# One pool of PSUM banks, pairs of 64 rows for the linear part and the sums, more queries turned by DMA

## The chip, the core and the metric

The kernel runs on one core of one Trainium2 chip. The core has five engines with a queue each: TensorE (PE, with PEld for its weight loads), VectorE (DVE), ScalarE (ACT), GpSimd (POOL) and SyncE (SP), which here issues almost all DMA transfers. An engine takes its queue in order. Matmuls write to PSUM, which has eight banks of 128 x 512 fp32; the other data lie in SBUF. The metric is the device time in microseconds of one execution; lower is better.

## What is computed

Attention through 49 agents, and a maxout layer behind it, in fp32 at the outside:

```python
B, N, C = (4, 12544, 128); n_agents = 49; d_ff = 768
def sm(a, b):
    s = scale * (a @ b.transpose(0, 2, 1))
    s = s - s.max(-1, keepdims=True)
    e = np.exp(s)
    return e / (e.sum(-1, keepdims=True) + 1e-09)
a2k = sm(agents, k)
agent_v = a2k @ v
q2a = sm(q, agents)
x = (q2a @ agent_v).reshape(B * N, C)
h = np.maximum(np.maximum(x @ w1, x @ w2), x @ w3)
out = h @ w_out
```

## The kernel before, in words

The kernel never forms x. For each batch b it works out `G` = agent_v times (w3-w1), (w2-w1) and (w1 w_out): 49 rows, kept twice, at partitions 0 to 48 and 64 to 112. The maximum of three products is then w1's product plus what two rectified differences add, and w1's product goes through the output layer as one linear part.

The queries come in 49 groups of 1024 (the last one takes two tiles of each batch). Steps have names, with the group s in them:

- `ql.s`, `qc.s`: SP loads q, POOL casts it to bf16. Then q is turned, either by `qt.s` (eight transposes on PE into PSUM) and `qe.s` (DVE copies that to SBUF), or by `qd.s` (one transposing DMA on SP). The set `TURNED` says which groups use `qd`.
- `sc.s`, `ex.s`: scores against the agents (two matmuls of 64 columns of the array each), and ACT's exponential, `e.s`: two halves of 49 rows, for even and odd tiles.
- `su.s`, `re.s`: PE sums the exponentials, DVE takes the reciprocals.
- for each of six parts f of the hidden layer: `u.s.f` and `v.s.f` on PE (two matmuls of 49 rows each, one per half, side by side in the array), `a.s.f` on ACT (relu of u), `x.s.f` on DVE (maximum of v and a, into `r`). For f = 4 ACT does both.
- `li.s.o`: the linear part of output tile o, opening its bank; `p.s.o.f`: four matmuls per part f and output tile o; `ov.s.o` on DVE scales by the reciprocals; `st.s` on SP stores.

For batches 1 to 3 the keys and values come in 11 chunks each, worked off between the query groups, about one a group until group 33: `kl`, `vl` load, `kc`, `vc` cast on POOL, `kt` turns by DMA, `ks` and `kx` make scores and exponentials, `kv` the weighted sum, `va` adds up. Batch 0 is done ahead of group 0, and there PE turns the keys.

The order of all steps is written out in the table `ORDER`, and `run` issues them in that order; each engine's queue follows from it. A number behind a name gives the place of its tile. PSUM is divided in two: `UV`, three tiles of two banks, for u, v and the early work; and `OM`, two tiles of one bank, for the turned q, the scores, the sums, the K chunks and the output tiles. The waits are placed by the framework.

In the profile L558 is u and v, L571, L565 and L568 are ACT's relus, L574 is DVE's maximum, L592 is p, L582 is li, L545 is su, L533 is sc, L523 is qt, L527 is qe, L599 is ov, L454 is every transposing DMA, L359 and L376 are ks and kv.

## Time and profile before

| | us |
|---|---|
| median of 3 runs (451.83 to 452.58) | 452.12 |
| profiled execution, span from first to last instruction | 449.8 |
| PE, DVE, ACT, POOL busy in it | 423.7, 402.8, 395.1, 169.4 |
| first hidden matmul (u of group 0) | 42.0 |

The profiled execution's own time beyond its span isn't given; the median of the runs lies 2.3 us over the span. Busy times are sums of records, and records of one engine overlap: matmuls flow through the array behind one another, and a busy engine isn't one at its limit. A row of a group has its line, engine, operation, tiles, shapes and count, then busy time and mean ns of one, then the idle time ahead of it. A tile mode, below, is the shape in which the array is used: all 128 rows, two halves of 64 rows, or two halves of 64 columns.

### The profile page before, as it was taken

The numbers are of one execution on the slowest core, as the hardware profiler recorded it, in microseconds if no ns is written. First come the engines' busy times: TensorE is split into PE (matmuls) and PEld (weight loads), VectorE is DVE, ScalarE is ACT, GpSimd is POOL, SyncE is SP. The second block draws the span as 40 slices with busy tenths as digits, with TensorE's granted clock in tenths as the row PEclk, the third lists the DMA queues.
The fourth block names the chain that finished last, engine by engine and source line by source line (L and its number), as shares of the span: only waits on it lengthen the run. The fifth ranks groups of instructions, "written<-read, shape, count | busy, mean of one in ns | idle before, by whom it ended". The sixth has DMA issues, their size and how long they took to land.

```text
span 449.8 us, 13103 instructions
## 1 busy us (share of the span) xinstructions
PE 423.7 (94%) x5388; PEld 274.0 (61%) x5388; DVE 402.8 (90%) x512; ACT 395.1 (88%) x461; POOL 169.4 (38%) x176
## 2 busy tenths in 40 slices
PE   0778899999999999999999999999999999999996
PEld 0654466666665666666666666666666655565675
DVE  1335999999999999999999999999999999999986
ACT  1459999999988999999989999999889899999983
POOL 1641645455676372464363263453402110100000
PEclk9989999999999999999999999999999999999999
DMA  8999999999999998999969799498608685327142
GB/s 311 409 408 387 326 373 310 263 394 316 340 320 274 392 216 223 408 273 318 406 200 324 216 350 226 141 314 336 212 6 230 191 221 129 96 103 178 48 177 107
DMA packets 80150, 117.80 MB, mean 262 GB/s; under 512 B 53527, under 2 KB 56283, under 8 KB 80091
## 3 DMA queue, kind: packets, MB, share of 16 engines
q1 hardware_dynamic: 79888, 116.87, 83.6%
q8 instruction: 42, 0.69, 0.6%
q14 instruction: 17, 0.14, 0.1%
q10 hardware_dynamic: 203, 0.10, 0.1%
HBM read 78.74 MB, written 25.69 MB: 232 GB/s over the span
## 4 chain that ended last, share of the span: by engine, by line
PE 73%; DMA 12%; DVE 6%; POOL 2%; ACT 2%; SPq 2%; issue 2%; POOLq 0%; DVEq 0%
PE UV L558 29%; PE OM L592 27%; DMA LD<-in_k_dram 6%; PE OM L582 5%; DMA LD<-in_v_dram 4%; DVE R L574 4%; PE OM L523 3%; PE OM L533 3%; PE OM L376 2%; DMA out_dram<-OS 2%; PE OM L359 2%; DVE OS L599 1%; SPq L454 1%; ACT AS L571 1%; ACT VB L333 1%
## 5 line engine op out<-in xcount | busy, mean ns | idle before, releaser
L574 DVE TENSOR_TENSOR R<-UV,AS 128x1024 bf16<-128x1024 f32 x245 | 293.4, 1219 | 11.4 <-PE UV L558 5.3
L571 ACT ACTIVATE AS<-UV 128x1024 bf16<-128x1024 f32 x245 | 246.7, 1023 | 18.3 <-PE UV L558 11.7
L558 PE MATMUL UV<-EQ,G 49*128 49x512 bf16 (+1 forms) x1248 | 178.5, 368 | 2.1 <-DVE R L574 1.3
L592 PE MATMUL OM<-wo_bf,R 128*128 128x128 bf16 x2352 | 179.8, 219 | 0.0
L592 PEld LDWEIGHTS <-R 128*128 128x128 bf16 x2352 | 139.7, 98 | 39.5 <-issue 37.3
L558 PEld LDWEIGHTS <-G 49*128 49x128 bf16 x1248 | 58.7, 93 | 63.9 <-issue 23.8
L517 POOL CAST QB<-LD 128x1024 bf16<-128x1024 f32 x49 | 50.8, 1040 | 111.9 <-DMA LD<-in_q_dram 50.6
L599 DVE TENSOR_TENSOR OS<-OM,RC 128x512 f32<-128x512 f32 x98 | 67.3, 686 | 2.6 <-PE OM L592 1.4
L335 POOL CAST KB<-LD 128x1152 bf16<-128x1152 f32 (+2 forms) x45 | 49.7, 1116 | 40.6 <-DMA LD<-in_k_dram 35.9
L335 POOL CAST VB<-LD 128x1152 bf16<-128x1152 f32 (+1 forms) x33 | 37.3, 1137 | 40.4 <-DMA LD<-in_v_dram 24.3
L568 ACT ACTIVATE R<-UV 128x1024 bf16<-128x1024 f32 x49 | 50.1, 1022 | 2.5 <-PE UV L558 1.7
L565 ACT ACTIVATE UV<-UV 128x1024 f32<-128x1024 f32 x49 | 49.9, 1019 | 2.3 <-DVE R L574 1.2
L582 PE MATMUL OM<-G,EQ 128*128 128x256 bf16 x196 | 37.9, 275 | 0.0
L474 POOL TENSOR_TENSOR EA<-EA,EK 128x441 f32<-128x441 f32 x27 | 27.6, 1023 | 18.5 <-ACT EK L365 18.1
L539 ACT ACTIVATE EQ<-OM 128x512 bf16<-128x512 f32 x49 | 29.4, 601 | 1.0 <-PE OM L533 0.9
L527 DVE COPY QT<-OM 128x1024 bf16<-128x1024 bf16 x38 | 26.0, 684 | 1.1 <-PE OM L523 1.0
L347 DVE COPY KT<-UV 128x1152 bf16<-128x1152 bf16 (+1 forms) x12 | 8.2, 700 | 18.2 <-PE UV L342 18.2
L523 PE MATMUL OM<-ident,QB 128*128 128x128 bf16 x304 | 23.7, 222 | 0.6 <-POOL QB L517 0.6
L582 PEld LDWEIGHTS <-EQ 128*128 128x128 bf16 x196 | 12.3, 97 | 15.9 <-issue 15.2
L523 PEld LDWEIGHTS <-QB 128*128 128x128 bf16 x304 | 18.5, 99 | 4.3 <-issue 2.6
L359 PEld LDWEIGHTS <-KT 128*128 128x128 bf16 x392 | 14.3, 98 | 10.0 <-issue 5.5
L533 PE MATMUL OM<-QT,agT 128*64 128x512 bf16 (+1 forms) x104 | 20.2, 393 | 0.0
(67 smaller groups left out, 196.4 us busy)
## 6 DMA issues: line engine op xcount, KB each, us to landing
LD<-in_q_dram SPq DMA_DIRECT2D x48, 512.0 KB, 6.6
out_dram<-OS SPq DMA_DIRECT2D x48, 512.0 KB, 6.3
LD<-in_k_dram SPq DMA_DIRECT2D x40, 576.0 KB, 7.8
LD<-in_v_dram SPq DMA_DIRECT2D x40, 576.0 KB, 9.4
LD<-in_k_dram SPq DMA_DIRECT2D x3, 512.0 KB, 6.0
LD<-in_v_dram SPq DMA_DIRECT2D x3, 512.0 KB, 11.4
LD<-in_moe_w_dram SPq DMA_DIRECT2D x6, 192.0 KB, 8.4
KT<-KB SPq DMA_TRANSPOSE x33, 6.7
```

What stands on the lines that cost most here:

```text
L335: (self.nc.gpsimd if eng == POOL else self.nc.vector).tensor_copy(out=out, in_=src)
L517: return lambda: self.nc.gpsimd.tensor_copy(out=self.t[f"qb.{s}"], in_=self.t[f"q.{s}"][:, :GT, :])
L523: self.nc.tensor.transpose(t[:, j * P:(j + 1) * P], self.t[f"qb.{s}"][:, j, :], self.ident)
L533: self.nc.tensor.matmul(self.t[f"qs.{s}"][h * H:(h + 1) * H, jj * P:(jj + pairs) * P], self.agT[:, b, :], self.t[f"qT.{s}"][:, 2 * jj + h: ...
L558: self.nc.tensor.matmul(t[:, h, jj * P:(jj + pairs) * P], self.t[f"G{b}"][h * H:h * H + A, c + f * P:c + (f + 1) * P], self.t[f"e.{s}"][h ...
L565: return lambda: self.nc.scalar.activation(self.t[f"u.{s}.{f}"], self.t[f"u.{s}.{f}"], AF.Relu)
L568: return lambda: self.nc.scalar.activation(self.t[f"r.{s}.{f}"], self.t[f"u.{s}.{f}"], AF.Relu)
L571: return lambda: self.nc.scalar.activation(self.t[f"a.{s}.{f}"], self.t[f"u.{s}.{f}"], AF.Relu)
L574: return lambda: self.nc.vector.tensor_tensor(out=self.t[f"r.{s}.{f}"], in0=self.t[f"v.{s}.{f}"], in1=self.t[f"a.{s}.{f}"], op=ALU.max)
L582: self.nc.tensor.matmul(self.t[f"o.{s}.{o}"][:, i * 2 * C:(i + 1) * 2 * C], self.t[f"e.{s}"][:, jj * P:(jj + 1) * P], self.t[f"G{of[jj]}"] ...
L592: self.nc.tensor.matmul(self.t[f"o.{s}.{o}"][:, c:c + C], self.t[f"r.{s}.{f}"][:, h, jj * P:(jj + 1) * P], self.wo_bf[:, f, :], start=Fals ...
L599: self.nc.vector.tensor_tensor(out=self.t[f"os.{s}"][:, j:j + 4, :], in0=self.t[f"o.{s}.{o}"].rearrange("p (j c) -> p j c", c=C), in1=self ...
```

## The change

1. PSUM is one pool `PS` of eight banks. A tile of u or v takes any two banks with a fixed distance (also 2 and 3, or 4 and 5), the others one bank.
2. Output tile o holds the tiles of parity o instead of the first or the last four, so that `p.s.o.f` reads one half of `r` alone. The tiles are opened by whichever step comes first, and the order fills one and then, mostly, the other.
3. The linear part `li.s` is one step of eight matmuls: the two halves of 49 rows side by side, each into its own output tile. `G` loses 128 columns of zeros for that. The sums are two steps `su.s.0` and `su.s.1`, of 49 rows and one column each; the second waits until the first has ended, as both write one bank.
4. `TURNED` has 22 groups instead of 11: 22, 25, 28 and 30 to 48.
5. The order is new, with another rule for the waits: the kernel works out itself which semaphores a step must wait for (`Plan.waits`), leaves out what an earlier wait implies, and puts all but one of a step's waits into instructions of their own. A helper records all instructions, so the changed kernel's rows all stand under L377. Steps `kr`, `fo.i` and `rs0` are parts of former steps, and the products for G come in halves of 384 columns.

Mode changes of the array, counted over PE's whole order: 569 before, 620 after. Instructions that only wait: on ACT 357 and 63, on DVE 309 and 133, on PE 6 and 100.

```diff
-C31, C21, C1O, WC = 0, DFF, 2 * DFF, 2 * DFF + 2 * C
+C31, C21, C1O, WC = 0, DFF, 2 * DFF, 2 * DFF + C
-TURNED = range(38, 49)
+TURNED = (22, 25, 28, *range(30, 49))
-SLOTS = {"UV": 3, "OM": 2, "LD": 13, "QB": 3, "KB": 3, "VB": 4, "KT": 3, "QT": 3, "EQ": 4, "EK": 4, "AS": 3,
+SLOTS = {"PS": 8, "LD": 13, "QB": 3, "KB": 3, "VB": 4, "KT": 3, "QT": 3, "EQ": 4, "EK": 4, "AS": 3,
...
-        add(f"su.{s}", PE, em.sums(s, m, not h), mm(GT // 2, 2), after=[f"ex.{s}"] + ([f"ks{b}.{g}" for b in range(1, B)
+        su = plan.tile("PS", f"su.{s}")
+        for h in range(2):
+            add(f"su.{s}.{h}", PE, em.sums(s, h), mm(GT // 2, 1), mode=ROW, after=[f"ex.{s}", "ones"], use=[su, f"e.{s}"], sides={su: h}, half=h)
...
-            add(f"li.{s}.{o}", PE, em.out_linear(s, o), mm(2, 256), after=[f"ex.{s}"] + lin, new=[("OM", f"o.{s}.{o}")], use=[f"e.{s}"] + gs)
+        add(f"li.{s}", PE, em.out_linear(s), mm(4, 128), mode=ROW, after=[f"ex.{s}"] + lin, use=both + [f"e.{s}"] + gs, sides=straight)
+                    add(f"p.{s}.{o}.{f}", PE, em.out_hidden(s, o, f), mm(4, 128), after=made[s, f][o] + ["cwo"], use=[both[o], f"r.{s}.{f}"])
...
+    def sums(self, s, h):
+        def fn():
+            t, rows = self.t[f"su.{s}"], slice(h * H, h * H + A)
+            for jj in range(GT // 2):
+                c = 4 * h + jj
+                self.nc.tensor.matmul(t[:, c:c + 1], self.t[f"e.{s}"][rows, jj * P:(jj + 1) * P], self.ones_bf[rows, :1],
+                                      start=self.first[f"su.{s}"] == self.now and jj == 0, stop=True, skip_group_check=True)
+        return fn
...
+    def out_linear(self, s):
+        def fn():
+            of = [p[0] for p in parts_of(s) for _ in range(p[4])]
+            for jj in range(GT // 2):
+                for h in range(2):
+                    rows = slice(h * H, h * H + A)
+                    self.nc.tensor.matmul(self.t[f"o.{s}.{h}"][:, jj * C:(jj + 1) * C], self.t[f"e.{s}"][rows, jj * P:(jj + 1) * P],
+                                          self.t[f"G{of[jj]}"][rows, C1O:], start=self.opens(s, h) and jj == 0, stop=True,
+                                          skip_group_check=True)
+        return fn
+
+    def out_hidden(self, s, o, f):
+        def fn():
+            for jj in range(GT // 2):
+                self.nc.tensor.matmul(self.t[f"o.{s}.{o}"][:, jj * C:(jj + 1) * C], self.t[f"r.{s}.{f}"][:, o, jj * P:(jj + 1) * P],
+                                      self.wo_bf[:, f, :], start=self.opens(s, o) and jj == 0, stop=True, skip_group_check=True)
+        return fn
...
+    def run(self, plan, order, place, tc):
...
+        waits, told, at, self.first = plan.waits(order, place)
+        for name in order:
+            o = plan.ops[plan.index[name]]
+            for x in waits[name][:-1]:
+                who, value = mark[x]
+                self.queues[o["eng"]].wait_ge(sems[who], value)
+            made.clear()
+            self.now = name
+            o["fn"]()
+            for x in waits[name][-1:]:
+                who, value = mark[x]
+                made[0].wait_op(sems[who], value, "sem-ge")
...
-kl0.5/0 prep kl0.0/1 kl0.9/2 kl0.1/3 kl0.6/4 vl0.0/5 vl0.11/6 ql.0/7 kl0.2/8 kl0.10/9 kl0.7/10 kc0.1/0 vl0.5/11 kc0.9/1 kt0.1/0
+kl0.11/12 kl0.10/0 agl id0 ql.0/1 qc.0/1 kl0.6/2 kl0.9/3 ones agc kc0.10/2 id kc0.6/0 kl0.4/8 kl0.2/1 agt/4 vl0.4/4 prep
```

PE's queue in the middle of the program, where a K chunk, the sums of one group and the linear part of the group ahead of it stand together. EQ is `e`, G0 the products of batch 0, R7 a tile of `r`; `sel` picks the two halves. Before, each load of weights is a row of its own:

```order
L359 MATMUL OM1_2715<-agT_77,KT2_2365 128x49
L545 LDWEIGHTS EQ0_2702
L545 MATMUL OM1_2715<-sel_79,EQ0_2702 128x2
...
L582 LDWEIGHTS EQ1_2317
L582 MATMUL OM0_2729<-G0_646,EQ1_2317 128x256
...
L592 LDWEIGHTS R7_2573
L592 MATMUL OM0_2729<-wo_bf_86,R7_2573 128x128
```

All of it uses the array at full height. After, a matmul and its load are one row, `x4` counts equal rows, and ps is the pool:

```order
L377 MATMUL ps_76<-QT1_104,agT_69 64x512 x2
L377 MATMUL ps_76<-wo_bf_72,R12_129 128x128 x4
L377 MATMUL ps_76<-ones_bf_66,EQ2_108 128x1 x4
L377 MATMUL ps_76<-EQ2_108,G1_144 128x512 x2
L377 MATMUL ps_76<-ones_bf_66,EQ2_108 128x1 x4
L377 MATMUL ps_76<-EQ2_108,G1_144 128x512 x4
L377 MATMUL ps_76<-G1_144,EQ1_107 128x128 x8
L377 MATMUL ps_76<-wo_bf_72,R8_125 128x128 x4
```

The two halves of the sums now stand on both sides of one hidden pair, and the linear part (128x128 x8) at the end of a run of hidden pairs, in their tile mode.

DVE's queue around group 30, where the first of the consecutive newly turned groups is used. Before:

```order
L465 TENSOR_TENSOR VA_4904<-OM_5876,VA_4904 128x49
L550 RECIPROCAL RC_5947<-OM_5876 128x8
L599 TENSOR_TENSOR OS_5852<-OM_5869,RC_5595 128x512
L574 TENSOR_TENSOR R_5965<-UV_5955,AS_5932 128x1024
L527 COPY QT_5992<-OM_5976 128x1024
L574 TENSOR_TENSOR R_6005<-UV_5998,AS_5906 128x1024
```

After, in the same place:

```order
L377 RECIPROCAL RC_130<-ps 128x8
L377 TENSOR_TENSOR R_121<-ps,AS_116 128x1024
L377 TENSOR_TENSOR OS_134<-ps,RC_132 128x4x128
L377 TENSOR_TENSOR R_120<-ps,AS_114 128x1024
L377 TENSOR_TENSOR VA_147<-ps,VA_147 128x49
L377 TENSOR_TENSOR OS_134<-ps,RC_132 128x4x128
```

The copy of the turned q is gone; maxima, scalings, sums and reciprocals remain.

SP's queue where the last K chunks of batch 3 are turned. Before:

```order
L454 DMA_TRANSPOSE KT_5775<-KB_5748 128x9x128
L325 DMA LD_5807<-in_k_dram 128x1024
L513 DMA LD_5814<-in_q_dram 128x1024
L513 DMA LD_5823<-in_q_dram 128x1024
L325 DMA LD_5835<-in_v_dram 128x1152
L454 DMA_TRANSPOSE KT_5847<-KB_5649 128x9x128
```

After:

```order
L377 DMA_TRANSPOSE KT_102<-KB_93 128x9x128
L377 DMA_TRANSPOSE QT_103<-QB_90 128x8x128
L377 DMA_TRANSPOSE KT_101<-KB_94 128x9x128
L377 DMA_TRANSPOSE QT_105<-QB_91 128x8x128
L377 DMA out_dram<-OS_142 128x1024
L377 DMA_TRANSPOSE QT_104<-QB_90 128x8x128
```

Transposes of q stand between those of K, and loads and stores behind them.

More of the change, by code (lines that the diff above doesn't have):

```diff
@@ L76, in parts_of, with lane @@
+    def lane(self, o, place, first):
+        if not o["use"]:
+            return "AG"
+        t = [x for x in o["use"] if first[x] == o["name"]] or o["use"]
+        cls = self.tiles[t[0]]
+        return f"{cls}{place[t[0]][0]}" + ("b" if cls == "LD" and first[t[0]] != o["name"] else "")
 def parts_of(s):
@@ L96, in mm @@
     t = n * max(cols / 2400 + 0.0025, 0.0253)
-    return t, t + 0.235
+    return t, t + 0.2
 def act(cols):
@@ L200, in graph @@
-        add(f"nr{b}", DVE, em.normalise(b, m), (0.5, 0.62), after=[f"to{b}", f"va{r}"], new=[("KR", f"kr{b}"), ("G", f"G{b}")],
-            use=[m, f"va{b}"], bank=m)
-        for name, c0, c1, eng in (("a", C31, C31 + DFF, ACT), ("c", C21, C21 + DFF, DVE), ("l", C1O, WC, ACT)):
+            use=[m, f"es{b}", f"e{r}"])
+        held = [f"gp{x}" for x in "abcd"] + ["gl"] if b == 2 else [f"gp{x}{b - 2}" for x in "abcdl"] if b > 2 else []
+        add(f"kr{b}", DVE, em.reciprocal_of(b, m), (0.25, 0.3), after=[f"to{b}"], new=[("KR", f"kr{b}")], use=[m])
@@ new lines, in graph @@
+            if f != FI:
+                for z, h in halves["v"]:
+                    v = f"v.{s}.{f}{z}"
+                    two = (1.136, 1.26) if h is None else (0.6, 0.72)
+                    add(v, PE, em.hidden(v, s, f, C21, True, h), pe, mode=ROW, after=[f"ex.{s}"] + needs("c", "d"),
+                        new=[("PS", v, 3 if h is None else 1)], use=[e] + gs, half=h)
+                    add(f"x.{s}.{f}{z}", DVE, em.max_second(v, s, f, h), two,
+                        after=[v] + [f"a.{s}.{f}{y}" for y, i in halves["u"] if i is None or h is None or i == h],
+                        use=[v, f"a.{s}.{f}", plan.tile("R", f"r.{s}.{f}")])
@@ L286, in __init__ @@
         self.w1T = const.tile([P, NF, P], BF16, name="w1T")
[L287 to L294 removed]
+        self.wall = const.tile([P, WC], BF16, name="wall")
+        self.ps = pools["psum"].tile([P, SLOTS["PS"], 512], FP32, name="ps")
```

812 lines of the change are left out of this document (458 added, 354 removed).

## The prediction

> **What bounds the kernel now.** I read the engines' shares first, then the busy time by stage, then the chain of work by stage, and last the order of TensorE in time, because a share near 100% says little on an engine whose matmuls overlap.
>
> ```profile
> span 449.8 us, 13103 instructions
> PE 423.7 (94%) x5388; PEld 274.0 (61%) x5388; DVE 402.8 (90%) x512; ACT 395.1 (88%) x461; POOL 169.4 (38%) x176
> ```
>
> Three engines look almost equally full. The table by stage (columns: stretch, its length, busy time of PE, weight loads, DVE, ACT, POOL, clock, DMA share, GB/s) doesn't part them either:
>
> ```profile
> 60.00:150.00 90.00, 88.43 (x1160) 57.43 (x1157) 85.60 (x109) 82.49 (x98) 52.37 (x53) 1.00 1.09 328
> 240.00:330.00 90.00, 89.99 (x1198) 59.02 (x1195) 88.17 (x113) 85.23 (x101) 38.47 (x40) 1.00 0.81 247
> 330.00:360.00 30.00, 29.74 (x334) 18.32 (x331) 29.26 (x34) 27.43 (x33) 5.20 (x5) 1.00 0.56 161
> 360.00:430.00 70.00, 69.71 (x744) 40.22 (x743) 67.09 (x74) 67.32 (x75) 5.17 (x5) 1.00 0.51 139
> ```
>
> DVE's 88.17 of 90 us is too high a reading: three maxima in a row took 3.49 us as one run, 1.16 each, while a single one has 1.219 in its group, so the records overlap by some 0.06 to 0.08 us each.
>
> ```profile
> 199.18 3.49 DVE L574 TENSOR_TENSOR R<-UV,AS 128x1024 bf16<-128x1024 f32 x3
> L574 DVE TENSOR_TENSOR R<-UV,AS 128x1024 bf16<-128x1024 f32 x245 | 293.4, 1219 | 11.4 <-PE UV L558 5.3
> L527 DVE COPY QT<-OM 128x1024 bf16<-128x1024 bf16 x38 | 26.0, 684 | 1.1 <-PE OM L523 1.0
> ```
>
> The chain of work decides it. From 240 to 330 us it is PE and nothing else; from 360 to 430 us, where q comes turned by DMA, some 13% of it lies on DVE, ACT and issue.
>
> ```profile
> by line: PE UV L558 38.8%; PE OM L592 35.6%; PE OM L582 7.1%; PE OM L523 5.8%; PE OM L533 4.1%; PE OM L376 3.8%; PE OM L359 3.2%; PE OM L545 1.2%; PE OM L491 0.3%; PE OM L493 0.2%; issue 0.0%
> by line: PE UV L558 40.3%; PE OM L592 34.3%; DVE R L574 6.9%; PE OM L582 6.5%; PE OM L533 4.3%; ACT AS L571 3.0%; issue 2.1%; DVE OS L599 1.6%; PE OM L545 1.4%; DVEq L574 0.0%
> ```
>
> So PE's starts in one period give the prices (PE in order of time: start, length, line, tile, count; the next row's start minus this one's is what a row costs):
>
> ```profile
> 254.31 0.61 PE L523 MATMUL OM<-ident,QB 128*128 128x128 bf16 x8
> 254.85 0.83 PE L558 MATMUL UV<-EQ,G 49*128 49x512 bf16 x6
> 255.62 1.07 PE L592 MATMUL OM<-wo_bf,R 128*128 128x128 bf16 x16
> 256.61 0.41 PE L533 MATMUL OM<-QT,agT 128*64 128x512 bf16 x2
> 256.95 0.82 PE L558 MATMUL UV<-EQ,G 49*128 49x512 bf16 x6
> 257.71 0.39 PE L582 MATMUL OM<-G,EQ 128*128 128x256 bf16 x2
> 257.94 0.39 PE L592 MATMUL OM<-wo_bf,R 128*128 128x128 bf16 x4
> 258.16 0.39 PE L359 MATMUL OM<-agT,KT 128*128 128x49 bf16 x9
> 258.39 0.38 PE L592 MATMUL OM<-wo_bf,R 128*128 128x128 bf16 x4
> 258.70 0.61 PE L558 MATMUL UV<-EQ,G 49*128 49x512 bf16 x4
> ...
> 259.71 0.24 PE L545 MATMUL OM<-sel,EQ 128*128 128x2 bf16 x4
> 259.88 0.39 PE L558 MATMUL UV<-EQ,G 49*128 49x512 bf16 x2
> ```
>
> A pair of 49-row matmuls over 512 columns costs 0.22 (the run of 6 is 0.22 longer than that of 4). Four out-products cost 0.22 (257.94 to 258.16), so 16 cost 0.88; but from 255.62 to 256.61 it was 0.99. The 0.11 left is a change of tile mode, and the three pairs from 254.85 to 255.62 (0.77 for 0.66) say the same. Turning q costs 0.54 less one change, 0.43. A half of the linear part costs 0.23 (257.71 to 257.94), 0.46 per group. The four sums have length 0.24, a single one 0.164, so they follow each other at 0.025, 0.10 per group. With PE's chain at 98 to 100%, what PE is spared or given there is time.
>
> ```profile
> L545 PE MATMUL OM<-sel,EQ 128*128 128x2 bf16 x196 | 11.9, 164 | 0.0
> 437.91 0.84 PE L558 MATMUL UV<-EQ,G 49*128 49x128 bf16 x24
> L558 PE MATMUL UV<-EQ,G 49*128 49x128 bf16 x96 | 3.7, 217 | 0.0
> ```
>
> **The change part by part.**
>
> *Linear part in pairs.* 98 x 0.23 = 22.5 us go. In their place stand 4 pairs of 49 rows by 128 columns per group. The last group's hidden layer already has that shape: 24 matmuls in 0.84, one of them 0.217, so 11 steps in 0.62, 0.056 per pair. 49 x 4 x 0.056 = 11.0 us. Term: -11.5.
>
> *Sums in halves.* Eight one-column matmuls instead of four of two columns. No row shows a narrow matmul of 49 rows; between 0.025 each (the full-height row) and 0.056 (the pair of 128 columns) I take 0.025, as the width is nearest to that: 8 x 0.025 = 0.20 against 0.10, +4.9 us; upper end +17. The halves write one bank, so the second waits for the first to end; in 31 groups only one pair (0.22) stands between them, against 0.164 for the matmul to end. Between 0 and 31 x 0.05; I take +0.5.
>
> *Changes of tile mode.* Counting in both orders, which list all of PE's work, the mode changes 569 times before and 620 times after. 51 x 0.11 = +5.6 (0.10 to 0.12: +5.1 to +6.1).
>
> *Eleven more groups turned by DMA.* PE loses 11 x 0.43 = 4.7 us, DVE 11 x 0.684 = 7.5 us. What this is worth is read from the rate of the groups (ACT's first relus, 5 per group):
>
> ```profile
> L571 ACT ACTIVATE AS<-UV 128x1024 bf16<-128x1024 f32 x56 | 56.7, 1024 | 3.8 <-PE UV L558 2.3
> L571 ACT ACTIVATE AS<-UV 128x1024 bf16<-128x1024 f32 x47 | 47.2, 1022 | 2.0 <-PE UV L558 1.3
> ```
>
> The first row is 240 to 330 us: 11.2 groups, 8.04 each. The second is 360 to 430 us: 9.4 groups, 7.45 each. Without the K chunk (two runs of 9 matmuls, 0.23 each by 258.16 to 258.39) the first would be 7.58, so turning by DMA has so far bought 0.13 per group rather than 0.43, since DVE and ACT come into the chain. Bounds -1.4 and -4.7; I take -3.0, the middle, as the first stage's groups have nothing else in their chain. The cost on the other side: SP issues 11 more transposes, and the casts on POOL (49 in both) and the loads of q stay.
>
> ```profile
> L454 SPq DMA_TRANSPOSE KT<-KB x33: 1233/2805/8161, 46.8 to 315.1; - x33
> L454 SPq DMA_TRANSPOSE QT<-QB x11: 1231/1232/3414, 336.9 to 407.7; - x11
> KT<-KB SPq DMA_TRANSPOSE x33, 6.7
> QT<-QB SPq DMA_TRANSPOSE x11, 3.3
> POOL QB L517 <- DMA QT<-QB: 20.2, 4, 10.4
> ```
>
> Between 1.2 and 2.8 us each on SP's queue, 14 to 31 us over the 125 us of groups 22 to 37; K's and V's loads and the stores stand behind them. The queue runs groups ahead, and the DMA share falls from 1.09 to 0.81 and 0.56 by then: 11 x 3.3 = 36 us more of transfers at most still fit. Cost 0 while that cover lasts. If it goes, PE stands before the scores, as it runs in order.
>
> *Waits.* Semaphores are now placed by the kernel's own rule. On ACT and DVE the instructions that only wait fall from 357 and 309 to 63 and 133; on PE they rise from 6 to 100. Such a wait on PE took 0.051:
>
> ```profile
> L523 PEldq EVENT_SEMAPHORE  x3: 51/51/51, 56.0 to 126.4; - x3
> ```
>
> 94 of them cost between 0 (PE's queue is ahead) and 4.8 us; I take a third, +1.6.
>
> *One pool.* A hidden tile may take any pair of the eight banks instead of one of three. What this can return is PE's idle time and the part of the chain off PE: 13.6% of 70 us in the late stage is 9.5 us, of the earlier stages 1.6 us by their table. So between 0 and -11; the new order also has less of PE's work to hide DVE behind. I take -1.5.
>
> *Start and end.* First hidden matmul at 42.0 us before:
>
> ```profile
> L558 PE MATMUL UV<-EQ,G x1248: 213/376/387, 42.0 to 442.8; 49*128 49x512 bf16 x165, 49*128 49x128 bf16 x14
> ```
>
> K, V, the weights' halves and q's first group are loaded ahead of it in both, in another order; 0, bounds -2 and +2.
>
> Sum: -11.5 + 4.9 + 0.5 + 5.6 - 3.0 + 1.6 - 1.5 = -3.4 us. The profiled span of 449.8 becomes 446.4. The runs' median of 452.12 lies 2.3 above that span; with the same 2.3 the forecast is 448.7 us. Its own range, with the bounds of its small terms (turning -4.7 to -1.4, waits 0 to 4.8, pool -5 to 0) is 443 to 451.
>
> **The rivals.**
>
> *The late stage closes up (faster, near 441).* With free choice of banks the 9.5 us off PE in the late stage go, and turning pays its full 4.7: -11.5 + 4.9 + 5.6 - 4.7 - 5.5 = -11.2. For it: DVE is spared 7.5 us. Against it: DVE and ACT stay within 5% of PE there.
>
> *The transposes come late (slower).* Place: SP's queue in groups 22 to 37, where K's last chunks are still loaded. For it: K's transposes landed in 6.7 us and held SP for up to 8.2; POOL has waited 20.2 us for q's to free a buffer. Against it: the shares above, and PE hardly waited for one. Price: each late one holds PE by up to the 3.4 us that landing in 6.7 instead of 3.3 adds. Two eat the gain; four late ones give 448.7 + 13.6 = 462.
>
> *Narrow matmuls of one half don't overlap (slower).* A weight load took 0.096 where the narrow matmul follows at 0.025. If each of a half's four loads had to wait, a group's sums would cost 8 x 0.096 = 0.77, +33 instead of +4.9: 477 us. It decides against the change from 0.034 per matmul on. For it: no row has this shape. Against it: at full height the loads overlap:
>
> ```profile
> L545 PEld LDWEIGHTS <-EQ 128*128 128x128 bf16 x196 | 9.1, 96 | 2.7 <-issue 2.7
> 259.66 0.20 PEld L545 LDWEIGHTS <-EQ 128*128 128x128 bf16 x4
> ```
>
> Four loads of 0.096 lie in 0.20 us, though all use the same rows. The Trainium skill, "TensorE: Matmul & The Clock Gate", Part 3, says that a weight load overlaps running matmuls only when its row group differs. By that rule the sums would run as in this rival; the trace disagrees at full height, and no run yet shows one half alone.
>
> *The weight loads wait too (slower).* After the change a matmul and its load are one instruction with one wait. If a third of 12 x 49 hidden pairs paid a load of 0.093 behind its wait, it would be +18 and 467. Against it: where a load came right ahead of its matmul, that started 0.01 us later.
>
> ```profile
> L558 PEld LDWEIGHTS <-G 49*128 49x128 bf16 x1248 | 58.7, 93 | 63.9 <-issue 23.8
> 195.31 0.11 PEld L582 LDWEIGHTS <-EQ 128*128 128x128 bf16 x2 [0.23 <-issue]
> 195.32 0.39 PE L582 MATMUL OM<-G,EQ 128*128 128x256 bf16 x2
> ```
>
> *No change.* More mode changes (0.12) and waits at 0.051 bring the sum to zero: 452.
>
> **How the numbers follow.** 0.2% of 452 us is 0.9 us, about what a measurement of this kernel tells from nothing. Forecast 0.45, late stage closing up 0.12, no change 0.08, late transposes 0.14, narrow halves 0.08, waiting loads 0.13 (of the last three most lands under 460). Faster 0.57, same 0.08, slower 0.35. The range from 440.5 to 460 leaves out some 3% below and 12% above.
>
> **What would show it.** Right: the linear part's runs of 8 at some 0.22 from start to start, sums of 4 at 0.1, mode changes still 0.11, a period near 8.0 us up to group 29 and 7.5 from 30 on, PE's chain at 95% or more from 150 to 300 us. Wrong: PE waiting for QT or KT, sums at 0.05 or more per matmul, a first hidden matmul later than 44 us, or an idle PE ahead of hidden matmuls with DVE and ACT idle too.

## The result, and the profile after

The changed kernel takes 455.06 us (median of seven runs, six of 453.49 to 457.28 and one far off, 717.51; without that one 454.93) and the one before, on the same chip, 452.52 (451.81 to 452.93): a ratio of 1.0061, interval 1.0033 to 1.0089. It is slower, by 0.6%. The forecast was 448.7, faster; 455.06 lies inside the range, on the wrong side.

First of the page of the kernel after: span, and busy time of each engine.

```profile
span 455.4 us, 13250 instructions
PE 428.9 (94%) x5692; PEld 267.0 (59%) x5692; DVE 396.9 (87%) x500; ACT 393.1 (86%) x464; POOL 169.3 (37%) x176
```

DVE lost 5.9 us of work and PE's records gained 5.2; which is little to go by, since a slow clock lengthens records. So I split the span in three: up to the end of group 1 (its second scaling on DVE), from there to the end of group 48, and the rest.

| profiled execution | before | after |
|---|---|---|
| first hidden matmul | 42.0 | 44.9 |
| end of group 1 | 68.0 | 73.7 |
| end of group 1 to end of group 48 | 378.3 | 377.1 |
| last scaling to the end of the span | 3.5 | 4.6 |

The whole loss, 5.7 us here, has come about by the end of group 1: 2.9 of it are there at the first hidden matmul, and 2.8 come between it and the end of group 1, 28.8 us where it was 26.0. The middle, where the forecast had its gain, gave 1.2 us; the end took 1.1. The profiled execution after is the slowest of its runs but the one far off (457.28), so of its 5.6 us only 2.5 stand in the medians. (The time beyond the span, which the runs list too, is 1.9 us and not the 2.2 of the kernel before, so the spans differ by some 2.9.)

What happens before the end of group 1 is in the table by stage (stretch, length, busy time of PE, weight loads, DVE, ACT, POOL, granted clock, DMA share, GB/s). Before:

```profile
42.00:48.00 6.00, 4.55 (x43) 2.17 (x42) 5.62 (x8) 5.23 (x8) 3.94 (x4) 1.00 1.04 386
48.00:54.00 6.00, 5.70 (x63) 3.06 (x61) 5.36 (x6) 5.64 (x9) 2.99 (x3) 1.00 1.12 282
54.00:60.00 6.00, 6.00 (x80) 3.89 (x77) 5.61 (x8) 5.86 (x7) 3.62 (x4) 1.00 1.11 326
```

After:

```profile
42.00:48.00 6.00, 5.00 (x40) 2.17 (x40) 4.11 (x12) 3.89 (x6) 2.48 (x3) 0.50 1.06 387
48.00:54.00 6.00, 5.74 (x29) 1.67 (x26) 4.49 (x5) 4.42 (x6) 3.88 (x4) 0.50 0.98 228
54.00:60.00 6.00, 6.00 (x68) 3.88 (x66) 4.04 (x5) 4.02 (x7) 3.33 (x3) 0.65 1.01 401
```

PE is as busy in both, but after it has 137 matmuls in 18 us and not 186: the granted clock is 0.50, 0.50 and 0.65. The record of the clock shows half speed from 41.12 to 58.19 us, 17.07 us, which is five stretches of 3.41. DVE and ACT, which wait for PE there, fall from between 5.2 and 5.9 to between 3.9 and 4.5 of 6 us. Cut along the clock's own stretches, the same table for the changed kernel begins one stretch ahead of the half speed:

```profile
37.70:41.12 3.42, 2.08 (x35) 1.27 (x34) 0.00 (x0) 3.42 (x6) 0.00 (x0) 1.00 1.03 395
41.12:44.53 3.41, 1.95 (x27) 1.04 (x23) 3.04 (x10) 1.92 (x3) 0.00 (x0) 0.50 1.09 369
44.53:47.95 3.42, 3.15 (x20) 1.18 (x18) 1.76 (x5) 2.80 (x5) 2.43 (x3) 0.50 1.02 403
47.95:51.36 3.41, 3.23 (x17) 1.01 (x15) 3.05 (x3) 1.83 (x4) 2.78 (x3) 0.50 0.87 215
51.36:54.78 3.42, 3.34 (x19) 1.37 (x20) 2.22 (x2) 3.32 (x5) 1.15 (x1) 0.50 1.09 277
54.78:58.19 3.41, 3.41 (x24) 1.67 (x22) 2.03 (x4) 1.84 (x3) 2.06 (x2) 0.50 1.01 402
```

PE was busy for 2.08 of 3.42 us ahead of the half speed, and its fifth stretch was the first in which PE was busy throughout. The largest hole ahead of it, 1.29 us up to 39.78, is a wait for an exponential on ACT, which stood there behind a cast of V; waits for DVE and for the last casts of V follow (ACT's rows, then PE's, in order of time; in brackets the wait ahead and what ended it):

```profile
38.10 1.20 ACT L377 ACTIVATE VB<-LD 128x1152 bf16<-128x1152 f32 x1
39.15 0.57 ACT L377 ACTIVATE EK<-ps 128x441 bf16<-128x441 f32 x1
39.57 3.31 ACT L377 ACTIVATE VB<-LD 128x1152 bf16<-128x1152 f32 x3
39.78 0.36 PE L377 MATMUL ps<-EK,ones_bf 128*128 128x441 bf16 x1 [1.29 <-ACT EK L377]
41.97 0.54 PE L377 MATMUL ps<-EK,VB 128*128 128x49 bf16 x9 [0.73 <-DVE KR L377]
42.93 0.55 PE L377 MATMUL ps<-EK,VB 128*128 128x49 bf16 x9 [0.43 <-ACT VB L377]
```

For the middle, the same stages that the prediction showed, and the chain of work by line for 240 to 330 and 360 to 430 us:

```profile
60.00:150.00 90.00, 89.63 (x1253) 57.05 (x1249) 85.99 (x111) 82.91 (x97) 46.82 (x48) 1.00 1.04 311
240.00:330.00 90.00, 89.66 (x1220) 55.75 (x1217) 84.94 (x106) 84.86 (x101) 41.56 (x43) 1.00 1.03 284
360.00:430.00 70.00, 69.61 (x838) 40.75 (x836) 67.04 (x74) 66.54 (x75) 6.08 (x6) 1.00 0.41 114
by line: PE ps L377 95.3%; DVE R L377 2.6%; ACT AS L377 1.1%; DVE OS L377 0.8%; issue 0.4%
by line: PE ps L377 90.2%; ACT AS L377 7.3%; issue 1.5%; ACT ps L377 0.7%; ACT R L377 0.5%
```

Between 240 and 330 us the chain was PE alone before; now 4.5% of it, 4 us, lies on DVE and ACT.

### The profile page after: what moved, and what is told of

Read it like the earlier page. It is cut to its first block, busy times and chain, and to the rows that moved or that the text cites. A ratio compares the mean times of both kernels' runs of the same rounds, so it can differ in the third digit from the quotient of the medians.

```text
span 455.4 us, 13250 instructions
## 1 busy us (share of the span) xinstructions
PE 428.9 (94%) x5692; PEld 267.0 (59%) x5692; DVE 396.9 (87%) x500; ACT 393.1 (86%) x464; POOL 169.3 (37%) x176
## 4 chain that ended last, share of the span: by engine, by line
PE 86%; DVE 4%; ACT 4%; issue 3%; DMA 1%; POOL 1%; POOLq 0%; DVEq 0%; SPq 0%
PE ps L377 86%; DVE R L377 3%; ACT VB L377 2%; ACT AS L377 1%; DMA LD<-in_k_dram 1%; DVE KT L377 1%; DVE OS L377 1%; ACT EK L377 1%; DVE QT L377 0%; POOL KB L377 0%; POOL QB L377 0%; ACT w_bf L377 0%; ACT ps L377 0%; ACT G L377 0%; ACT R L377 0%
## 5 line engine op out<-in xcount | busy, mean ns | idle before, releaser
L377 DVE TENSOR_TENSOR R<-ps,AS 128x1024 bf16<-128x1024 f32 x245 | 294.7, 1220 | 15.8 <-PE ps L377 10.1
L377 ACT ACTIVATE AS<-ps 128x1024 bf16<-128x1024 f32 x245 | 245.3, 1024 | 20.3 <-PE ps L377 17.1
L377 PE MATMUL ps<-EQ,G 49*128 49x512 bf16 (+1 forms) x1248 | 196.4, 375 | 2.0 <-DVE R L377 0.4
L377 PE MATMUL ps<-wo_bf,R 128*128 128x128 bf16 x2352 | 180.7, 220 | 0.1
L377 PEld LDWEIGHTS ps<-wo_bf,R 128*128 128x128 bf16 x2352 | 133.2, 98 | 58.8 <-issue 52.1
L377 POOL CAST QB<-LD 128x1024 bf16<-128x1024 f32 x49 | 50.6, 1041 | 148.6 <-DMA LD<-in_q_dram 57.1
L377 PEld LDWEIGHTS ps<-EQ,G 49*128 49x128 bf16 x1248 | 56.1, 93 | 59.3 <-ACT AS L377 10.7
L377 DVE TENSOR_TENSOR OS<-ps,RC 128x512 f32<-128x512 f32 x98 | 66.9, 683 | 1.6 <-PE ps L377 0.9
L377 POOL CAST KB<-LD 128x1152 bf16<-128x1152 f32 (+2 forms) x45 | 49.9, 1116 | 35.6 <-DMA LD<-in_k_dram 20.8
L377 ACT ACTIVATE ps<-ps 128x1024 f32<-128x1024 f32 x49 | 49.8, 1016 | 3.9 <-PE ps L377 3.1
L377 ACT ACTIVATE R<-ps 128x1024 bf16<-128x1024 f32 x49 | 50.1, 1023 | 1.1 <-PE ps L377 0.3
L377 POOL CAST VB<-LD 128x1152 bf16<-128x1152 f32 (+1 forms) x33 | 37.2, 1137 | 29.0 <-DMA LD<-in_v_dram 20.8
L377 POOL TENSOR_TENSOR EA<-EA,EK 128x441 f32<-128x441 f32 x27 | 27.6, 1024 | 14.2 <-ACT EK L377 13.8
L377 ACT ACTIVATE EQ<-ps 128x512 bf16<-128x512 f32 x49 | 29.3, 599 | 2.8 <-PE ps L377 2.5
L377 ACT ACTIVATE EK<-ps 128x441 bf16<-128x441 f32 (+2 forms) x45 | 23.5, 532 | 7.0 <-PE ps L377 7.0
L377 ACT ACTIVATE VB<-LD 128x1152 bf16<-128x1152 f32 (+1 forms) x12 | 12.2, 1055 | 16.3 <-DMA LD<-in_v_dram 13.9
L377 PEld LDWEIGHTS ps<-ones_bf,EQ 49*128 49x128 bf16 x392 | 18.3, 93 | 11.5 <-DVE OS L377 0.7
L377 PE MATMUL ps<-ones_bf,EQ 49*128 49x1 bf16 x392 | 24.1, 163 | 0.1
L377 DVE COPY KT<-ps 128x1152 bf16<-128x1152 bf16 (+1 forms) x12 | 8.2, 701 | 15.0 <-PE ps L377 14.8
L377 PE MATMUL ps<-QT,agT 128*64 128x512 bf16 (+1 forms) x104 | 20.6, 402 | 0.0
L377 DVE COPY QT<-ps 128x1024 bf16<-128x1024 bf16 x27 | 18.4, 680 | 2.1 <-PE ps L377 1.9
L377 PE MATMUL ps<-EK,VB 128*128 128x49 bf16 x392 | 17.7, 187 | 1.9 <-ACT VB L377 1.1
```

The lines of the kernel that those rows point to most:

```text
L377: i = call(*args, **named)
```

## The experiments

All runs in one table; ratios are against runs of the kernel before on the same chip (medians 452.38 to 452.98). "1 to 48" is the middle stretch above. "Half clock" is the mean number of 3.41-us stretches at half speed per run, from the mean clock and the span that each run lists: (1 - clock) x 2 x span / 3.413. Profile columns come from one execution each, and the first row's last column from 29 runs beside `a_start`.

| kernel | median us | ratio (interval) | first hidden | end of group 1 | 1 to 48 | half clock |
|---|---|---|---|---|---|---|
| before | 452.5 | 1 | 42.0 | 68.0 | 378.3 | 1.4 |
| after | 455.06 | 1.0061 (1.0033, 1.0089) | 44.9 | 73.7 | 377.1 | 4.8 |
| a_start | 452.20 | 0.9983 (0.9963, 1.0003) | 42.1 | 70.2 | 377.1 | 2.2 |
| a_warm | 452.14 | 0.9975 (0.9951, 0.9998) | 42.7 | 69.0 | 377.0 | 1.5 |
| a_warm_b | 452.49 | 1.0003 (0.9981, 1.0024) | 44.2 | 70.4 | 377.0 | 2.0 |
| a_warm2 | 452.82 | 1.0005 (0.9989, 1.0021) | 42.7 | 68.6 | 377.8 | 1.8 |
| b_cold | 454.23 | 1.0021 (1.0002, 1.0041) | 41.6 | 68.7 | 379.0 | 4.3 |
| a_lifull | 473.07 | 1.0421 (1.0385, 1.0457) | | | 392.8 | 4.8 |
| a_unturn | 471.33 | 1.0392 (1.0349, 1.0434) | | | 393.4 | 4.8 |
| a_turn | 457.10 | 1.0108 (1.0058, 1.0158) | | | 380.6 | 3.4 |
| a_li1 | 454.99 | 1.0042 (1.0012, 1.0072) | | | 377.4 | 4.9 |
| b_li1 | 450.46 | 0.9946 (0.9923, 0.9969) | | | 375.4 | 1.1 |
| a_ov | 454.21 | 1.0014 (0.9985, 1.0042) | | | 376.7 | 3.6 |
| a_act | 454.71 | 1.0036 (1.0004, 1.0067) | | | 375.9 | 4.6 |
| a_all | 452.52 | 0.9995 (0.9971, 1.0020) | | | 375.0 | 3.7 |
| a_tail | 456.86 | 1.0089 (1.0055, 1.0122) | | | 377.6 | 6.1 |
| a_fix | 453.59 | 1.0016 (0.9990, 1.0043) | 44.1 | 69.3 | 377.0 | 1.7 |
| a_best | 453.29 | 1.0004 (0.9982, 1.0026) | 42.3 | 70.2 | 377.1 | 1.9 |
| a_best2 | 453.28 | 1.0006 (0.9987, 1.0025) | 42.3 | 71.0 | 377.2 | 1.8 |

**The start: its order, or the clock?** Three kernels. `a_start` takes the table's words up to the first hidden step from the kernel before. `a_warm` adds eleven warm-up steps (`wm`: matmuls whose result nobody reads) where PE stood, and changes nothing else. `b_cold` takes six warm-ups from the kernel before. A piece of each:

```diff
# a_start
-kl0.11/12 kl0.10/0 agl id0 ql.0/1 qc.0/1 kl0.6/2 kl0.9/3 ones
+kl0.5/0 id0 agl id ones
...
# a_warm
-SPARE = 8
+SPARE = 19
-ql.1/12 vc0.3/3 to0.7 su.0.0
+ql.1/12 vc0.3/3 wm.8/5 wm.9/4 wm.10/0 wm.11/2 wm.12/1 to0.7 su.0.0
-vc0.1/2 kv0.7 kv0.1 nr0/0
+vc0.1/2 wm.13/5 wm.14/4 wm.15/0 kv0.7 wm.16/2 kv0.1 nr0/0
# b_cold, against the kernel before
-SPARE = 8
+SPARE = 2
-to0.10 to0.11 wm.2/2 wm.3/0 wm.4/1 rc0/0
+to0.10 to0.11 rc0/0
```

> The changed kernel with the order of the kernel before up to the first hidden matmul (loads, V casts, cast of w1, warm-up matmuls), the new order behind it. Theory S (the loss lies in the start: V's casts end 2.9 us later on ACT, and TensorE's clock is halved for the next 17 us): first hidden matmul at 42 us instead of 44.9, mean clock 0.99 or more, end of group 0 near 60 us instead of 65.5, time near 449 (455.1 less 2.9 and less 3.2). Rival P (the loss lies in the steady part: the one pool of banks and the new order stall PE in small pieces, and a later start is made up for behind it): 454 to 455.

> The changed kernel with 11 more warm-up matmuls in PE's gaps between 38.5 and 44.9 us, nothing else. Theory S: the clock is not halved behind 41 us, the first hidden matmul stays at 44.9 (within 0.3), groups 0 and 1 take 3 us less, time near 452. Rival P: the half clock costs nothing because DVE and ACT set the rate there: 455, whatever the clock does.

> The kernel before without its last 6 warm-up matmuls (38.1 to 41.3 us). Theory S: the clock is halved for some 17 us behind 41 to 42 us as in the changed kernel, time 452.5 + 3.2 = 455.7. Rival P: 452.5.

The clock, by stage, in the execution with more warm-ups, where one stretch at half speed is left (49.73 to 53.14 us):

```profile
42.00:48.00 6.00, 5.09 (x43) 1.87 (x39) 5.34 (x10) 5.37 (x9) 3.78 (x4) 1.00 0.98 378
48.00:54.00 6.00, 5.47 (x49) 3.03 (x49) 4.54 (x5) 4.62 (x7) 2.57 (x3) 0.72 1.00 231
```

and in the kernel before with fewer:

```profile
36.00:42.00 6.00, 4.39 (x46) 2.36 (x46) 3.30 (x9) 5.01 (x9) 0.00 (x0) 0.60 1.05 385
42.00:48.00 6.00, 5.91 (x36) 2.57 (x35) 4.63 (x8) 4.26 (x5) 4.17 (x5) 0.54 1.04 386
```

Warm-ups alone take the loss away (452.14 against 455.06; as ratios 0.9975 against 1.0061), and taking them from the kernel before brings a third of it there (+0.21% of the 0.61%). The old order at the start takes it away too, though it brings the first hidden matmul back to 42.1 and shortens the half clock at once, so it doesn't tell the two apart. And its fill lost what it had won: group 1 ends at 70.2. There PE waits for a cast on POOL:

```profile
44.54 0.39 PE L377 MATMUL ps<-EQ,G 49*128 49x512 bf16 x2
46.22 0.51 PE L377 MATMUL ps<-wo_bf,w1T 128*128 128x128 bf16 x6 [1.29 <-POOL wo_bf L377]
```

**Again, and with still more warm-ups.** `a_warm_b` is `a_warm` unchanged, on another occasion; `a_warm2` has five more, also behind the first hidden matmul.

```diff
-a.0.0/0 u.0.2/3,4 qt.1/0 gvd
+a.0.0/0 u.0.2/3,4 wm.21/0 qt.1/0 gvd
-qc.2/0 v.0.4 gl/2
+qc.2/0 wm.22/2 wm.23/3 v.0.4 gl/2
```

> The changed kernel with 11 more warm-up matmuls again, beside the others of this call. If the halved clock is what separates the changed kernel from the kernel before: 452 again, 0.5 us under the kernel before, with one to two half-clock windows in each run.

> The same with five more warm-up matmuls in PE's gaps from 44 to 49 us, where the profile of the first showed one half-clock window (49.7 to 53.1). At 0.65 us per window of 3.4 us: 0.6 to 1.0 us under the first, 451.3, if no window is left. If the warm-ups delay the hidden matmuls by their own length: 452.5 or more.

In `a_warm_b` the first hidden matmul came at 44.2, almost as late as after the change, and the median is still that of the kernel before. From that matmul to the end of group 1 it took 26.2 us, as `a_warm` did (26.3) and not the 28.8 of the changed kernel: what these two groups lose is the clock's. The later start isn't free, though: that execution took 453.75 us and the profiled one of `a_warm` 452.49, and group 1 ended 1.4 us later. The start moves by itself: the first cast of V, which waits for the first loads, started at 14.57, 16.18 and 16.74 us in `a_warm`, `a_warm_b` and the changed kernel, whose orders agree up to there:

```profile
14.57 1.16 ACT L377 ACTIVATE VB<-LD 128x1152 bf16<-128x1152 f32 x1 [11.76 <-DMA LD<-in_v_dram]
```
```profile
16.18 1.16 ACT L377 ACTIVATE VB<-LD 128x1152 bf16<-128x1152 f32 x1 [13.36 <-DMA LD<-in_v_dram]
```
```profile
16.74 1.16 ACT L377 ACTIVATE VB<-LD 128x1152 bf16<-128x1152 f32 x1 [13.94 <-DMA LD<-in_v_dram]
```

The new order moves it too: from this cast to the first hidden matmul it is 28.0 to 28.2 us in all three, with or without warm-ups, and 25.6 in the kernel before, whose first cast of V starts at 16.36. In the eight profiled executions with the changed kernel's start and no added warm-ups the first hidden matmul comes at 44.4 to 45.1 us, in the six with the start of the kernel before at 41.3 to 42.3. What this is worth in the medians can't be read, as only profiles date the start.

Five more warm-ups bring no more; with no half clock left in the fill of the profiled execution (0.999), the time is 452.82. What a stretch of half clock costs: within the runs of one kernel, with 296 runs of all kernels taken together, time rises by 0.68 us per stretch (standard error 0.05). The changed kernel's own six hardly show a slope, as five of them list the same clock. The two kernels differ by 3.4 stretches, of which some 0.4 lie at the changed kernel's end, from 454.13 us on, where PE is done; at that slope the other 3 are worth some 2.0 of the 2.5 us. Between two profiles it was 0.9 per stretch: behind the first hidden matmul the changed kernel has 3.9 of them and `a_warm` one, and it took 2.5 us longer to the end of group 1. Between medians it was 0.9 too (`a_warm` against after, -2.9 us for 3.3; by the ratios 1.2) and 0.4 (`b_cold`, +1.25 for 2.9), on both sides of that slope. So the half clock is the cause of most of the loss, and its share is known to some 40%.

**The linear part.** Full height again, eight matmuls against zeros, in the same order:

```diff
-        add(f"li.{s}", PE, em.out_linear(s), mm(4, 128), mode=ROW, ...)
+        add(f"li.{s}", PE, em.out_linear(s), mm(8, 128), ...)
```

> The changed kernel with its linear part at full height (8 matmuls of 128 rows by 128 columns per group against a G padded with zeros), in the same places of the order. By the prediction's prices: 49 x (8 x 0.0558 - 0.224) = +10.9 us for the matmuls and 69 more changes of tile mode (689 for 620) x 0.11 = +7.6, together 455.1 + 18.5 = 473.6. If pairs of 64 rows are no cheaper than full height: 462.7. If the linear part is hidden behind DVE and ACT: 455.

The middle went from 377.1 to 392.8: +15.7. In its PE rows the eight cost 0.54 from start to start, with a change of mode in it:

```profile
201.32 0.61 PE L377 MATMUL ps<-G,EQ 128*128 128x128 bf16 x8
201.86 0.82 PE L377 MATMUL ps<-EQ,G 49*128 49x512 bf16 x6
```

In the changed kernel the pairs cost 0.23, the narrow sums 0.17 with a change of mode (rows of PE in order of time):

```profile
59.01 0.24 PE L377 MATMUL ps<-ones_bf,EQ 49*128 49x1 bf16 x4
59.18 0.40 PE L377 MATMUL ps<-wo_bf,R 128*128 128x128 bf16 x4
...
60.85 0.40 PE L377 MATMUL ps<-G,EQ 49*128 49x128 bf16 x8
61.08 0.38 PE L377 MATMUL ps<-EQ,G 49*128 49x512 bf16 x2
```

Then less of it: one of the four pairs per group in the changed kernel, half of the linear part in the one before, each leaving the rest of it out.

```diff
# a_li1, out_linear
-            for jj in range(GT // 2):
+            for jj in range(1):
# b_li1, the linear part of the kernel before
-            for i in range(2):
+            for i in range(1):
```

> The changed kernel with one of the four pairs of the linear part in each group; the other three are left out, so three quarters of the linear part is missing. PE is spared 49 x 3 x 0.056 = 8.2 us in the steady part and nothing else changes. If PE alone sets the rate, the stretch from group 1 to group 48 falls from 377.0 to 369. Rival: PE, DVE and ACT limit together, so that a saving on PE is paid out in part only: 372 to 375, with more stalls ahead of hidden matmuls.

> The kernel before with one of the two matmuls of each half of the linear part; the other is left out, so half of the linear part is missing. PE is spared 98 x 0.115 = 11.3 us. The prediction's premise (with PE's chain at 98 to 100%, what PE is spared is time): 452.5 - 11.3 = 441, the stretch from group 1 to group 48 falls from 378.3 to 367. Rival (DVE, ACT and the banks limit beside PE, and the chain only shows who came last): 449 to 452, as in the changed kernel, where 8.2 us less on PE gave nothing.

In `a_li1` its own steps took some 4 us less, and most of that was back within the next few operations of PE; the middle stayed (+0.3). In the kernel before, 11.3 us less of PE's work bought 2.9 of the middle, where the premise of the prediction had all of it. So in an order that is settled, work added to PE costs nearly its price (15.7 of 18.5 expected), and work taken away returns a quarter or nothing.

**Turning.** The eleven groups on PE again, and four more by DMA (with the warm-ups of `a_warm`):

```diff
# a_unturn
-TURNED = (22, 25, 28, *range(30, 49))
+TURNED = range(38, 49)
# a_turn
+TURNED = (22, 23, 25, 26, 27, 28, 29, *range(30, 49))
```

> The changed kernel with the 11 more groups (22, 25, 28, 30 to 37) turned on PE again: PE gets 11 x 0.447 and 4 changes of tile mode, +5.3 us, DVE 11 x 0.68 = +7.5 us. The prediction priced this at 3.0 with bounds 1.4 and 4.7. If PE alone sets the rate, the stretch from the end of group 1 to the end of group 48 (377.0 us in three starts) grows by 5.3; if DVE does, by up to 7.5; if transposes by DMA cost elsewhere what they save here, by 0 or less.

> The changed kernel with the 11 warm-up matmuls and four more groups (23, 26, 27, 29) turned by DMA. PE is spared 4 x (0.447 + two changes of tile mode at most), 1.8 to 2.7 us, DVE 4 x 0.68 = 2.7 us, SP gets four more transposes at a DMA share of 1.03 to 1.06. If DVE is the limit there: the stretch falls by 2 to 2.7 and the time from 452.1 to 449.8. If saving on an engine gives nothing in an order that was settled without it: 452. If the transposes collide with K's loads: PE waits for QT and the time is 453 or more.

(The steps `qt`, `qe` and `qd` stand in the table accordingly; in `a_unturn` the loads and casts of q around them stand in another order too.) Turned on PE again: +16.3 in the middle, of which the transposes are some 5. Much of the rest are waits ahead of inserted steps and hidden matmuls, eight of 0.7 to 1.3 us, such as

```profile
316.48 0.40 PE L377 MATMUL ps<-wo_bf,R 128*128 128x128 bf16 x4
317.71 0.62 PE L377 MATMUL ps<-ident,QB 128*128 128x128 bf16 x8 [0.83 <-DVE R L377]
```

so this run tells less what turning is worth than what it costs to put steps into an order settled without them. Four more groups by DMA cost 3.6 us in the middle. SP's queue, then DVE and PE, in order of time:

```profile
261.45 9.97 SPq L377 DMA_TRANSPOSE KT<-KB  x2
271.46 1.31 SPq L377 DMA_TRANSPOSE QT<-QB  x1
272.82 0.58 SPq L377 DMA_DIRECT2D out_dram<-OS  x1
277.73 0.69 DVE L377 TENSOR_TENSOR OS<-ps,RC 128x512 f32<-128x512 f32 x1 [2.12 <-DMA out_dram<-OS]
278.48 0.40 PE L377 MATMUL ps<-agT,KT 128*128 128x49 bf16 x9 [1.13 <-DVE OS L377]
279.61 0.61 PE L377 MATMUL ps<-EQ,G 49*128 49x512 bf16 x4 [0.73 <-DVE R L377]
```

Three transposes hold the queue for 11.3 us, a store behind them is issued at 272.82, and a scaling on DVE waits 2.12 us until a store has read its buffer. PE waits 1.13 us for the bank that this scaling frees, and 0.73 for the maxima behind it. So the place of the late-transposes rival, SP's queue, is right, but what came late was a store, not a turned q. These two waits and one of 0.59 for a cast on POOL are 2.5 of the 3.6 us. Behind them the clock fell to half for one stretch in the middle of the program (the table by stretches again):

```profile
277.52:280.93 3.41, 1.72 (x28) 1.02 (x28) 3.20 (x4) 1.67 (x3) 1.18 (x2) 1.00 1.07 396
280.93:284.35 3.42, 3.42 (x32) 2.20 (x31) 2.54 (x5) 2.75 (x4) 0.87 (x1) 0.50 0.99 327
```

At 0.68 us a stretch it can be part of the rest; that isn't shown.

With 22 turned groups no scaling between 150 and 330 us waited for a store, though there too two K transposes held SP, for 12.81 us from 253.12 (SP's row in `a_warm`):

```profile
253.12 12.81 SPq L377 DMA_TRANSPOSE KT<-KB  x2
```

**Which engine holds the middle?** Scalings over half the columns, the relu of one part in six over half its columns, and both with `a_li1`; each leaves the other half out.

```diff
# a_ov
-            self.nc.vector.tensor_tensor(out=self.t[f"os.{s}"][:, o::2, :], ...)
+            self.nc.vector.tensor_tensor(out=self.t[f"os.{s}"][:, o::2, :C // 2], ...)
# a_act
+        w = 256 if out.startswith("a.") and out.endswith(".0") else 512
```

> The changed kernel with the scaling of the output tiles on half of its columns (DVE spared about 98 x 0.27 = 26 us, by 0.6 for the whole; half of the output is left at zero). If DVE limits the steady part alone: 377.0 from group 1 to group 48 falls by 10 or more, down to what PE's work sets. If no engine does alone: by less than 4. If DVE isn't in it: nothing.

> The changed kernel with the first relu of each group (f = 0) on half of its columns (ACT spared 48 x 0.43 = 21 us; half of that hidden tile is left at zero). If ACT limits the steady part alone: 377.0 falls by 10 or more; if no engine does alone: by less than 4; if ACT isn't in it: nothing.

> The changed kernel with three cuts at once: one of four pairs of the linear part, half of the columns of the scalings and of the first relu of each group (three quarters of the linear part, half of the output and half of one hidden tile are missing). Alone they moved the stretch from group 1 to group 48 (377.0) by +0.4, -0.3 and -1.1 us. If PE, DVE and ACT limit together, the three cuts at once give more than their sum: PE's own cut of 4 us (0.234 to 0.168 per linear part, and 0.16 where the mode changes) comes back, and the stretch is 371 to 373. If the order or the banks limit and no engine does: 375 to 376, the sum of the three.

The middle fell by 0.4, 1.2 and, with all three cuts, some 2 us. The sum of the three alone, with the +0.3 of `a_li1`, is 1.3, so together they bought a little more than their sum, and far from the 4 to 6 us that were expected of engines full side by side. I take it that the order and the time from one engine to the next set the pace; that is argued by exclusion and no run shows it alone.

**The end.** The last nine stores of older groups went ahead, so that the last two find SP's queue empty.

```diff
-p.48.0.4 p.48.0.5 st.44 ov.48.0 st.47 ...
+p.48.0.4 p.48.0.5 ov.48.0 ...
```

> The changed kernel with only the last nine stores moved: each is issued as soon as its group is scaled, instead of five of them behind the hidden layer of the last group. Theory: from the last scaling to the end of the span 3.5 us as in the kernel before instead of 4.6, the rest of the trace unchanged, so the time falls by 1.1. Rival: the 4.6 are the last group's own four stores; then nothing changes.

The end stayed at 4.58 us, so older stores are not its cause. (The time rose, to 456.86, with 6.1 stretches of half clock.) Where it comes from: before, the first two stores of the last group start before the second scaling has ended (DVE's and SP's rows of the kernel before):

```profile
444.93 1.36 DVE L599 TENSOR_TENSOR OS<-OM,RC 128x512 f32<-128x512 f32 x2 [0.59 <-PE OM L592]
445.65 1.79 SPq L607 DMA_DIRECT2D out_dram<-OS  x4
```

In the changed kernel (here `a_warm`) they wait for both, as a scaling now fills every other column of all four:

```profile
444.67 1.36 DVE L377 TENSOR_TENSOR OS<-ps,RC 128x512 f32<-128x512 f32 x2 [0.49 <-PE ps L377]
446.06 1.82 SPq L377 DMA_DIRECT2D out_dram<-OS  x4
```

From the scalings' start it is 0.72 us before and 1.39 now, 0.67 of the 1.1.

**Versions meant to beat both.** `a_fix`: the warm-ups, the cast of w1 later, two casts of V shared with DVE, and the stores of `a_tail`. `a_best`: `a_start` with the product of w1 and wo moved behind the first maxima. `a_best2`: that and seven warm-ups.

```diff
# a_fix
-        m = n if n == KT else 2
+        m = 4 if g in (3, 7) else n if n == KT else 2
# a_best
-v.0.1/1,2 a.0.2/2 pl/5 qe.1/0 el v.0.0/6,7
+v.0.1/1,2 a.0.2/2 qe.1/0 v.0.0/6,7
-x.0.3/5 a.0.5/0 qc.2/0
+x.0.3/5 pl/2 a.0.5/0 el qc.2/0
```

> The changed kernel with the 11 warm-up matmuls, with the cast of w1 (0.74 us on ACT) behind the last V cast, with 5 of the 9 columns of V casts 3 and 7 on DVE, which is idle there (2 x 0.55 us off ACT), with the identity ahead of the first q cast on POOL, and with the last nine stores issued as soon as their groups are done. Theory S (start and tail are where the time lies): 452.1 of the warm-up run less 0.75, less 1.1, less 1.1 for the tail, 449.2. Rival D (the last V load, not ACT, sets the first hidden matmul): only the tail's 1.1, 451.0. Rival P (steady part): 452 to 455.

> The changed kernel with the start of the kernel before, and the product of w1 and wo moved back by some ten matmuls, behind which PE stood for 1.29 us waiting for wo. First hidden matmul near 42 us, no wait of 1.29 us at 45, from the first hidden matmul to the end of group 1 some 26 us instead of 28.1, from there on the same 377.0 and 4.6: span near 449.7, time near 451.5, 0.3% under the kernel before. If the start isn't the cause of the rest: 452.2 as without the move.

> The same with seven more warm-up matmuls in PE's gaps from 38 to 43 us. If the clock still halves in the run without them: 0.65 us less per window of 3.4 us, near 451. If it does not: the same, or later by what the warm-ups delay.

None is faster than both the kernel before and `a_warm`. In `a_fix` the last cast of V waited for its load instead of for ACT:

```profile
40.90 1.16 ACT L377 ACTIVATE VB<-LD 128x1152 bf16<-128x1152 f32 x1 [0.39 <-DMA LD<-in_v_dram]
```

In `a_best` the 1.29 us of POOL's cast became three waits for DVE's maxima, and group 1 still ends at 70.2:

```profile
46.77 0.61 PE L377 MATMUL ps<-EQ,G 49*128 49x512 bf16 x4 [0.46 <-DVE R L377]
47.84 0.61 PE L377 MATMUL ps<-EQ,G 49*128 49x512 bf16 x4 [0.47 <-DVE R L377]
49.09 0.82 PE L377 MATMUL ps<-wo_bf,w1T 128*128 128x128 bf16 x6 [0.64 <-DVE R L377]
```

## Why the prediction was wrong

Its sign was wrong by two of its terms: the start, put at nothing, cost more than the steps on PE gained, and the part from turning to the one pool gave 0.7 us instead of 2.9. I set steps on PE from start to next start, from the first hidden matmul to the last operation, in the kernel before against `a_warm`, whose clock was at half for one stretch only there:

| term of the sum | forecast | measured |
|---|---|---|
| linear part | -11.5 | -10.7 |
| sums, their wait for each other | +5.4 | +5.8 |
| changes of mode | +5.6 | +4.6 |
| turning, waits on PE, one pool | -2.9 | -4.5 + 3.8 = -0.7 |
| sum | -3.4 | -1.0 |
| start: first hidden matmul | 0 (-2 to +2) | +2.9 in the profile |
| groups 0 and 1, at half clock | not in the sum | +2.8 in the profile; by the slope half clock is some 2.0 of the medians' 2.5 |
| end | 0, in the start's bounds | +1.1 |

- **"Start and end ... 0, bounds -2 and +2" failed.** I compared what is loaded ahead of the first hidden matmul and did not ask how long the new order takes on ACT, when PE stands still there, and whether the clock answers. The +5.7 us of the profile lie outside the bounds; the medians' some 2.0 are at their edge, where the forecast had nothing. The sign it named, a first hidden matmul later than 44 us, came true (44.9). `a_warm_b` shows that its date is not all of the cause: with 44.2 but a clock that held for all but one stretch, group 1 ended at 70.4 and not at 73.7.
- **Turning, waits and one pool: right in its parts, wrong in its sum.** PE is spared 4.5 us by turning, as the price of 4.7 says. But I let 3.0 of it through and took another 1.5 from the pool. 3.8 us, among them what the one stretch of half clock in `a_warm` cost, came back as stalls: the chain from 240 to 330 us, all PE before, has 4.5% on DVE and ACT now, and the late stage still has 10% off PE. By the ends of the groups (each one's second scaling), the way from 1 to 22 took 178.5 instead of 177.5 us, from 22 to 38 128.8 instead of 132.8, from 38 to 44 44.5 instead of 46.9, and from 44 to 48, where most of that was given back, 25.3 instead of 21.1. The sign of a period near 8.0 us up to group 29 and 7.5 from 30 on failed: 8.4 us from group 1 to 29, and 8.1 from there to 37. `a_li1` shows the same on a smaller scale, and `b_li1` that the premise, what PE is spared is time, held for a quarter of the work even before the change.
- **The prices on PE were right.** The pairs run at 0.23 per group (forecast "some 0.22"), the four sums at 0.107 on average (forecast 0.1), and a change of mode takes 0.095 to 0.098 (forecast 0.11).
- **The rivals.** *Narrow halves don't overlap* is false: the rows above show 0.17 for four sums with a change of mode, where four loads of 0.093 in a row would be 0.37. *Weight loads wait* is false: the steps of the hidden pairs add up to 161.2 us before and 161.4 in `a_warm`. By the rule of the Trainium skill, "TensorE: Matmul & The Clock Gate", Part 3, that a weight load overlaps running matmuls only when its row group differs, the sums would have run in turn; the trace disagrees for one half alone too. *Late transposes* is false here; four groups on, SP's queue did cost time, by a store. *The late stage closes up* is false: PE's share of the chain there went from 86.8% (the five PE lines of the row before) to 90.2, no further. *No change* came nearest, for a reason it did not name: with the clock mostly held (`a_warm`, `a_warm_b`, `a_warm2`), the two kernels are within 0.3% of each other.
- **A sign that was no test.** PE's chain of at least 95% came true (97.0% from 150 to 300 us), and the gain did not: a sign that holds before as well as after tests nothing.

## What to carry to other kernels

Where PE waits in the fill, look at the granted clock of each stage before and after a change, cut PE's busy time along the clock's own stretches, and price an idle gap by the half-speed stretches that follow; a few matmuls that nobody reads can be worth more than the work saved later. In an order written out for engines that each take their queue in turn, a saving on one of them is worth what is left when the next waits have moved up (here a quarter or less), while added work costs nearly its price. A single profile can be at the end of its kernel's scatter: compare the parts of the span, and the medians, before telling a cause.
